# Threshold attention and a hard-swish projection on one core: both attention products of a quad end in one slot, and the last 64 keys are transposed by VectorE from 32 by 32 blocks

## Chip, cores and metric

The kernel runs on one core of a Trainium2 chip. Times are device microseconds of one execution. Five engines work side by side, each in its own fixed order of instructions: TensorE (PE, with its weight loads as PEld), VectorE (DVE), ScalarE (ACT), GpSimd (POOL) and SyncE (SP), which here only issues transfers.

## The reference

For each of 8 batches and 8 heads, with 576 tokens of 64 numbers:

```python
scores = scale * q @ k.T
thresh = max(scores) - tau                      # per row
scores = where(scores >= thresh, scores, -1e9)
attn = exp(scores - max(scores)); attn /= sum(attn) + 1e-9
x = attn @ v                                    # heads side by side: 4608 x 512
h = x @ w_in                                    # 512 -> 2048
out = (h * clip(h + 3, 0, 6) / 6) @ w_out       # 2048 -> 512
```

All inputs and the output are float32.

## The kernel before

**Tiling.** Two heads form a pair and four a quad; there are 16 quads. The 576 query rows of a head are four tiles of 128 and a rest of 64. A quad has 9 slots: slots 0 to 3 are the tiles of its first pair, 4 to 7 those of its second, and slot 8 has the rests of all four heads. The loop walks 144 slots in an order written out by hand (the scheduler is off), so what each engine does next is the order of these lines.

**A slot.** `scores` of a slot were issued at the end of the slot before, as 8 or 16 float32 matmuls into the two buffers of `ps_s` (tile `s` in the profile). VectorE takes the row maximum and moves the scores to SBUF (`sm_max`, line 277), GpSimd makes the bias (280), ScalarE masks (285) and exponentiates (290, one slot later), VectorE makes the reciprocal (293), GpSimd normalises to bf16 `pn` (298), and SP transposes `pn` by DMA to `pT` (slots 0 to 7) or `pR` (slot 8).

**Work put between.** To fill TensorE each slot also carries pieces of the projections of an earlier batch. `mm1` makes a piece of h (8 matmuls of width 256 or 320, line 353) in the single buffer of `ps_h`; its ReLU runs on ScalarE in slots 0, 1, 3, 5 (line 362) and on VectorE in the others (364), then VectorE's gate (370) writes `g`. Slot 8 has no `mm1`. `mm2_part` runs 4 of the 16 matmuls of an output tile (382, tile `o` in the single buffer of `ps_o`); every fourth part is followed by VectorE's eviction to `osb` (390) and a transfer. There is one part in each slot, none in slot 3, and two in slot 0 or 1.

**Attention products.** `av_main` (10 matmuls of width 512, lines 323 and 326, tile `av`) makes x for a pair from `pT`: for the first pair of a quad in slot 8, for the second in slot 3 of the next quad. `av_rest` (20 matmuls of width 64, tile `ar`) does the rest rows of a quad from `pR` in slot 4 of the next. Both end with a VectorE cast into `xT` (335, 343). Their PSUM bank comes from `bank`, which from slot 28 on always gives the single buffer of `ps_m`, shared with the transposes `tp` and `tr`.

**Keys and queries.** From the third batch on (quads 4 to 15) queries are loaded in 32 by 32 blocks and VectorE transposes them (222). Keys 0 to 511 are transposed by TensorE (213) and copied out by ScalarE (203). The last 64 keys of a quad's four heads lie in `kr`, loaded by two DMAs (107) in slot 6 for the quad after next; in slot 7 `transpose_rest` transposes them with one matmul (231, tile `tr`), and ScalarE moves the two halves to `kT`. Loads for a quad (`km`, `nq`, `kr`) leave SP's queue one step a slot in slots 4 to 8, between the DMA transposes.

Of the kernel before, what the change touches and what calls it, by code (L numbers as in the profile page):

```python
# [21 lines left out]
def kernel(  # L22
# [57 lines left out]
    def load_quad(quad):  # L80
        b, g = divmod(quad, 2)
        nat[quad] = (nat_pool.tile([P, 1152], F32, tag="nq", name="nq"),
                     nat_pool.tile([P, 4, 4, D], F32, tag="km", name="km"),
                     nat_pool.tile([P, 2 * D], F32, tag="kr", name="kr"))
        nq, km, kr = nat[quad]

        def main(dst, src, h, order):
            nc.sync.dma_start(out=dst[:, :, h, :], in_=src[b, 4 * g + h, 0:512, :].rearrange(order, t=4))

        def blocks_q(n, a, j):  # L90
            c = 32 * (2 * a + j)
            nc.sync.dma_start(out=nq[c:c + 32, n * S:(n + 1) * S].rearrange("p (k d) -> p k d", d=32),
                              in_=q[b, 4 * g + 2 * n + a, :, 32 * j:32 * j + 32].rearrange("(k r) d -> r k d", r=32))

        def load_q(n):
            if b < NB:
                for a in range(2):
                    main(nq[:, 0:1024].rearrange("p (t h d) -> p t h d", h=4, t=4), q, 2 * n + a, "(t p) d -> p t d")
            else:
                for a in range(2):  # L100
                    for j in range(2):
                        blocks_q(n, a, j)

        def rest():
            for dst, src in ((kr[:], k), (nq[:, 1024:1152], q))[0:2 if b < NB else 1]:
                for n in range(2):
                    nc.sync.dma_start(out=dst[64 * n:64 * n + 64, :].rearrange("p (h d) -> p h d", h=2),
                                      in_=src[b, 4 * g + 2 * n:4 * g + 2 * n + 2, 512:S, :].rearrange("h p d -> p h d"))

        for n in range(2):  # L110
            loads.append(lambda n=n: [main(km, k, 2 * n + a, "(p t) d -> p t d") for a in range(2)])
            loads.append(lambda n=n: load_q(n))
            if n == 0:
                loads.append(rest)
# [76 lines left out]
    def bank(name):  # L191
        nonlocal turn
        turn += 1
        if now < N2 and turn % 2:
            return ps_o.tile([P, 512], F32, tag="o", name=name)
        return ps_m.tile([P, 512], F32, tag="m", name=name)
# [29 lines left out]
        return lambda: copy_out(kT_of(pair)[:, 64:576], ps[:])  # L226

    def transpose_rest(quad):
        ps = bank("tr")
        nq, _, kr = nat[quad]  # L230
        nc.tensor.transpose(ps[:, 0:P], kr[:], identf[:])
        if by_pe(2 * quad):
            nc.tensor.transpose(ps[:, P:2 * P], nq[:, 1024:1152], identf[:])

        def evict():
            qT, kT = qkT[quad]
            both = ps[:].rearrange("p (w n t) -> p w n t", n=2, t=64)
            if by_pe(2 * quad):
                nc.vector.tensor_copy(out=qT[:, :, 512:S], in_=both[:, 1])
            copy_out(kT[0:64, :, S:S + 64], both[0:64, 0])  # L240
            copy_out(kT[64:P, :, 0:64], both[64:P, 0])
        return evict
# [66 lines left out]
    def pe_transpose(sl):  # L309
        ps = ps_h.tile([P, 2, 1024], BF16, tag="h", name="pt")  # L310
        ps = ps[:].rearrange("p a b -> p (a b)")[:, 0:2 * S].rearrange("p (c t) -> p c t", t=P)
        pn = sl.pn[:].rearrange("p a b -> p (a b)")
        for c in range(9):
            nc.tensor.transpose(ps[:, c, :], pn[:, c * P:(c + 1) * P], identb[:])
        return lambda: nc.vector.tensor_copy(out=sl.dst, in_=ps)
# [12 lines left out]
    def av_main(pair):  # L328
        b, hp = divmod(pair, NPAIR)
        if hp == 0:  # L330
            xT[b] = x_pool.tile([P, KI, S], BF16, tag="xT", name="xT")
        ps = bank("av")
        av(ps[:], pair, pts[pair], slice(0, 512))
        o0 = 64 if b % 2 else 0
        nc.vector.tensor_copy(out=xT[b][:, hp, o0:o0 + 512], in_=ps[:])  # L335

    def av_rest(quad):
        b, g = divmod(quad, 2)
        ps = bank("ar")
        for n in range(2):  # L340
            av(ps[:, n * 64:(n + 1) * 64], 2 * quad + n, ptr[quad], slice(n * 64, (n + 1) * 64))
        o0 = 0 if b % 2 else 512
        nc.vector.tensor_copy(out=xT[b][:, 2 * g:2 * g + 2, o0:o0 + 64],
                              in_=ps[:, 0:P].rearrange("p (a b) -> p a b", a=2))

    def mm1(item, pool=None):
        b, ni, c0, w = item
        hps = (pool or ps_h).tile([P, 2, 512], F32, tag="s" if pool else "h", name="h")  # L350
        for n in range(2):
            for ki in range(KI):
                nc.tensor.matmul(hps[:, n, 0:w], w_in_sb[:, ki, (ni + n) * P:(ni + n + 1) * P],  # L353
                                 xT[b][:, ki, c0:c0 + w], start=(ki == 0), stop=(ki == KI - 1))
        return hps[:, :, 0:w]
# [78 lines left out]
    for n, sl in enumerate(queue):  # L434
        quad, slot = sl.quad, sl.slot
        b, g = divmod(quad, 2)
        now = n
        if slot in (0, 4):
            pts[2 * quad + slot // 4] = pt_pool.tile([P, 9, 512], BF16, tag="pT", name="pT")
        if slot == 8:  # L440
            ptr[quad] = ptr_pool.tile([P, 9, P], BF16, tag="pR", name="pR")
        if quad == 0 and slot == 0:
            load_quad(1)
        if slot == (4 if quad else 8) and quad + 2 < NQUAD:
            load_quad(quad + 2)
        if slot == 0 and g == 1 and b + 1 < B:
            load_v(b + 1)
        if prev is not None:
            for i in range(2):
                sm_exp(prev, i)  # L450
        sm_max(sl)

        if slot != 8 and todo1:
            item, then = todo1.pop(0)
            h = mm1(item)
            r = mm1_relu(h, on_act=(slot in (0, 1, 3, 5)))
            mm1_gate(item, h, r)
            todo2.extend(then)
        copies = pe_transpose(queue[n - 2]) if n > 1 and queue[n - 2].on_chip else None
        if prev is not None:  # L460
            sm_recip(prev)
        if copies:
            copies()
        outs = []


        pieces = 0 if slot == 3 else 1
        if slot == 0:
            second = True
        if second and slot < 2 and len(todo2) > 1 and todo2[0][1] == todo2[1][1]:  # L470
            pieces, second = 2, False
        for _ in range(pieces):
            if todo2:
                bb, mt, part = todo2.pop(0)
                mm2_part(bb, mt, part)
                if part == 3:
                    outs += mm2_out(bb, mt, on_act=False)
        for i in range(2):
            sm_mask(sl, i)
        evict = None  # L480
        nxt = 2 * quad + 2
        if slot == (1 if quad else 2):
            evict = transpose_q(2 * quad + 1)
        elif slot == (2 if quad else 3):
            evict = transpose_k(2 * quad + 1)
        elif slot == 3 and quad > 0:
            av_main(2 * quad - 1)
        elif slot == 4 and quad > 0:
            av_rest(quad - 1)
            if quad % 2 == 0:  # L490
                todo1.extend(moe_of(quad // 2 - 1))
        elif slot in (5, 6, 7) and quad + 1 < NQUAD:
            if slot == 5:
                alloc_qk(quad + 1)
                evict = transpose_q(nxt)
            elif slot == 6:
                evict = transpose_k(nxt)
            else:
                evict = transpose_rest(quad + 1)
        elif slot == 8:  # L500
            av_main(2 * quad)
        if evict:
            evict()
        if n + 1 < len(queue):
            queue[n + 1].tiles = scores(queue[n + 1].quad, queue[n + 1].slot)
        if n < 8:
            warm_up(6)
        if prev is not None:
            sm_norm(prev)
        flush()  # L510
        late.extend(outs)
        start(loads, 1)
        if n < 4 or n > 12:
            start(vcasts, 1)
        if n > 3:
            start(casts, 1 if n < 24 else 2)
        prev = sl
# [24 lines left out]

    for item in todo1:
        rest1(*item)
    av_main(2 * last + 1)
    rest2()
    av_rest(last)
    for item in moe_of(B - 1):
        rest1(*item)
    rest2()  # L550
# [35 lines left out]
```

## Time and profile before

| What | us |
|---|---|
| Median of 8 runs | 562.63 (562.13 to 563.22) |
| Profiled execution | 562.28 |
| Its span | 560.5 |
| Quad 6, start to start of its scores | 30.12 |
| Quad 8 | 31.93 |
| Quad 13 | 32.68 |
| From the scores of the last slot to the end | 61.1 |

The span runs from the first to the last instruction of the profiled execution; the time of that execution has 1.8 us around it. The granted TensorE clock is 0.995 of full. Times in timelines count from the span's start. A line "A <- B" names the instruction that waited and what released it; "x8" counts merged instructions. Quads differ because of the widths of `mm1` and of where an output eviction falls.

### The profile page before, as it was taken

What the parts mean: (1) busy time and instruction counts of PE and PEld (TensorE: products, weight loads), DVE (VectorE), ACT (ScalarE), POOL (GpSimd) and SP (SyncE); (2) the same over time, 40 slices, a digit from 0 to 9 for tenths busy, and PEclk for the clock granted to TensorE, in tenths of its full rate; (3) what the DMA queues carried; (4) which work ended last, traced back from release to release, by engine and by line L of the source; (5) the groups of instructions that cost most, each with busy time, mean ns of one, the idle gap of its engine ahead of it and who ended that gap; (6) DMA issues with size and microseconds to landing.
All of it is one profiled execution on the core that took longest, in us unless ns stands there. A gap on an engine that the chain in (4) does not pass through costs nothing.

```text
span 560.5 us, 11593 instructions
## 1 busy us (share of the span) xinstructions
PE 530.4 (95%) x3815; PEld 308.4 (55%) x3856; DVE 424.4 (76%) x1040; ACT 470.0 (84%) x999; POOL 305.2 (54%) x646
## 2 busy tenths in 40 slices
PE   7898798799999999999999999999999999999997
PEld 5565355455555555655555555655555555654663
DVE  3687777687878798887978788887978788883440
ACT  3899899798888999899898999899888999983540
POOL 1878878864556555755556555754556555561000
PEclk9999899999999999999999999999999999999999
DMA  5989999986789877989699867977699866453102
GB/s 108 138 120 170 159 162 185 199 155 134 132 155 153 150 142 153 180 148 147 128 146 169 165 125 152 182 149 145 132 139 171 169 121 122 101 109 84 38 20 75
DMA packets 286204, 77.52 MB, mean 138 GB/s; under 512 B 269248, under 2 KB 281536, under 8 KB 286144
## 3 DMA queue, kind: packets, MB, share of 16 engines
q1 hardware_dynamic: 268736, 67.86, 65.5%
q0 software_dynamic: 17408, 8.92, 14.0%
q8 instruction: 30, 0.49, 0.4%
q14 instruction: 30, 0.25, 0.2%
HBM read 36.70 MB, written 9.44 MB: 82 GB/s over the span
## 4 chain that ended last, share of the span: by engine, by line
PE 55%; DVE 12%; ACT 10%; issue 4%; DMA 2%; SPq 2%; POOL 2%; DVEq 0%; POOLq 0%
PE h L353 17%; PE o L382 16%; PE s L256 15%; DVE s L277 5%; ACT s L285 4%; ACT s L290 3%; PE av L323 3%; DVE g L370 2%; DMA nq<-in_q_dram 2%; DVE r L364 2%; ACT r L362 2%; PE s L262 1%; PE tp L213 1%; POOL pn L298 1%; DVE osb L390 1%
## 5 line engine op out<-in xcount | busy, mean ns | idle before, releaser
L298 POOL TENSOR_SCALAR pn<-s,rinv 128x576 bf16<-128x576 f32 x288 | 211.6, 745 | 133.1 <-DVE rinv L293 58.4
L285 ACT ACTIVATE s<-s,bias 128x576 f32<-128x576 f32 x288 | 207.0, 766 | 35.7 <-POOL bias L280 34.6
L277 DVE TENSOR_SCALAR_CACHE_REDUCE s<-s 128x576 f32<-128x576 f32 x288 | 205.8, 752 | 40.4 <-PE s L256 30.5
L290 ACT ACTIVATE s<-s 128x576 f32<-128x576 f32 x288 | 192.7, 671 | 0.3
L256 PE MATMUL s<-kT,qT 64*128 64x288 f32 x1024 | 170.6, 430 | 5.9 <-DVE s L277 3.2
L353 PE MATMUL h<-xT,w_in_sb 128*128 128x320 bf16 (+1 forms) x1024 | 144.9, 287 | 5.9 <-DVE g L370 5.0
L382 PE MATMUL o<-w_out_sb,g 128*128 128x512 bf16 x535 | 133.5, 379 | 5.9 <-DVE osb L390 3.0
L353 PEld LDWEIGHTS <-w_in_sb 128*128 128x128 bf16 x1024 | 92.1, 97 | 68.8 <-issue 31.5
L256 PEld LDWEIGHTS s<-kT,qT 64*128 64x128 f32 x1024 | 93.9, 186 | 62.4 <-DVE s L277 24.9
L370 DVE SCALAR_TENSOR_TENSOR g<-r,h 128x512 bf16<-128x512 f32 (+1 forms) x128 | 96.4, 754 | 41.8 <-ACT r L362 39.9
L280 POOL TENSOR_SCALAR bias<-m 128x1 f32<-128x1 f32 x288 | 54.4, 189 | 67.6 <-DVE s L277 47.8
L382 PEld LDWEIGHTS <-g 128*128 128x128 bf16 x576 | 55.6, 98 | 58.2 <-issue 9.8
L362 ACT ACTIVATE r<-h,three 128x640 f32<-128x640 f32 (+1 forms) x74 | 54.4, 737 | 20.6 <-PE h L353 20.0
L290 ACT ACTIVATION_READ_ACCUMULATOR s<-s 128x1 f32 x288 | 54.2, 188 | 0.0
L364 DVE TENSOR_SCALAR r<-h 128x512 f32<-128x512 f32 (+1 forms) x54 | 40.5, 750 | 0.0
L390 DVE TENSOR_SCALAR osb<-o 128x512 f32<-128x512 f32 x31 | 21.0, 676 | 22.2 <-PE o L382 22.2
L323 PE MATMUL av<-pT,vm 128*64 128x512 bf16 x256 | 34.6, 393 | 2.1 <-ACT kT L203 2.0
L323 PEld LDWEIGHTS <-vm 128*64 128x64 bf16 x512 | 18.0, 111 | 25.3 <-issue 18.6
L293 DVE RECIPROCAL rinv<-rsum 128x2 f32<-128x2 f32 x144 | 23.0, 160 | 11.4 <-ACT s L290 10.1
L335 DVE CAST xT<-av 128x512 bf16<-128x512 f32 x32 | 21.8, 681 | 6.5 <-PE av L326 6.2
L277 DVE DVE_READ_ACCUMULATOR s<-s 128x1 f32 x288 | 23.9, 83 | 0.0
L388 ACT ACTIVATE osb<-o 128x512 f32<-128x512 f32 x5 | 3.0, 597 | 23.9 <-PE o L382 23.9
(42 smaller groups left out, 255.5 us busy)
## 6 DMA issues: line engine op xcount, KB each, us to landing
km<-in_k_dram SPq DMA_DIRECT2D x64, 128.0 KB, 3.1
out_dram<-osb SPq DMA_DIRECT2D x32, 256.0 KB, 2.4
nq<-in_q_dram SPq DMA_DIRECT2D x96, 72.0 KB, 2.9
vm<-in_v_dram POOLq DMA_DIRECT2D x16, 256.0 KB, 5.3
nq<-in_q_dram SPq DMA_DIRECT2D x16, 128.0 KB, 4.3
w_in_sb<-in_moe_w_in_dram POOLq DMA_DIRECT2D x16, 128.0 KB, 4.6
w_out_sb<-in_moe_w_out_dram POOLq DMA_DIRECT2D x16, 128.0 KB, 4.5
pT<-pn SPq DMA_TRANSPOSE x119, 3.4
```

What stands on the lines that cost most here:

```text
L256: nc.tensor.matmul(tiles[a][:, hf, 0:HALF], qT_of(pair)[a * 64:(a + 1) * 64, t * P:(t + 1) * P], keys(pair, a, hf), start=True, stop=True)
L277: nc.vector.tensor_scalar(out=sl.s[:, i, :].rearrange("p (a b) -> p a b", a=2), in0=ps[:, :, 0:HALF], scalar1=1.0, scalar2=None, op0=Alu.m ...
L280: nc.gpsimd.tensor_scalar(out=sl.bias[:, i:i + 1], in0=sl.m[:, i:i + 1], scalar1=-scale, scalar2=tau, op0=Alu.mult, op1=Alu.add)
L285: nc.scalar.activation(out=s, in_=s, func=Act.Prelu, bias=sl.bias[:, i:i + 1], scale=scale, alpha=REJECT)
L290: nc.scalar.activation(out=s, in_=s, func=Act.Exp, accum_out=sl.rsum[:, i:i + 1])
L298: nc.gpsimd.tensor_scalar(out=pn[:, i, :], in0=sl.s[:, i, :], scalar1=sl.rinv[:, i:i + 1], scalar2=1.0, op0=Alu.mult, op1=Alu.mult)
L323: nc.tensor.matmul(ps[a * 64:(a + 1) * 64, :], vm[:, 2 * hp + a, c * D:(c + 1) * D], pT[:, 5 * a + c, cols], start=(c == 0), stop=False)
L353: nc.tensor.matmul(hps[:, n, 0:w], w_in_sb[:, ki, (ni + n) * P:(ni + n + 1) * P], xT[b][:, ki, c0:c0 + w], start=(ki == 0), stop=(ki == KI ...
L362: nc.scalar.activation(out=r, in_=hps, func=Act.Relu, bias=three[:])
L364: nc.vector.tensor_scalar(out=r, in0=hps, scalar1=3.0, scalar2=0.0, op0=Alu.add, op1=Alu.max)
L370: nc.vector.scalar_tensor_tensor(out=gbuf[:, ni:ni + 2, c0:c0 + w], in0=r, scalar=6.0, in1=hps, op0=Alu.min, op1=Alu.mult)
L382: nc.tensor.matmul(o_ps[0], gbuf[:, ni, mt * P:(mt + 1) * P], w_out_sb[:, ni, :], start=(ni == 0), stop=(ni == NI - 1))
```

## The change

Four edits take effect together:

- From quad 3 on, `av_main` of the second pair moves from slot 3 to slot 4, and `av_rest` from the end of slot 4 to right behind it. Both stand ahead of the slot's `mm1`. `av_rest` no longer takes a bank of its own: it writes columns 384 to 511 of the second half of the buffer of `ps_h` that the same slot's `mm1` then fills in columns 0 to 255 or 0 to 319.
- The `mm2` part of slot 4 moves to slot 3, in the same quads.
- On VectorE the cast of `av` stands ahead of slot 4's ReLU, and the cast of `ar` behind its gate.
- In quads 4 to 15 `kr` is loaded in blocks by 8 DMAs of 32 partitions, and two VectorE transposes write the last 64 keys straight into `kT`; the matmul and ScalarE's two copies go.

```diff
+        def blocks_rest():
+            for a in range(2):
+                for j in range(2):
+                    c = 32 * (2 * a + j)
+                    for n in range(2):
+                        nc.sync.dma_start(
+                            out=kr[c:c + 32, 64 * n:64 * n + 64].rearrange("p (k d) -> p k d", d=32),
+                            in_=k[b, 4 * g + 2 * n + a, 512:S, 32 * j:32 * j + 32].rearrange("(k r) d -> r k d", r=32))
+
         def rest():
+            if b >= NB:
+                return blocks_rest()
...
     def transpose_rest(quad):
+        nq, _, kr = nat[quad]
+        if not by_pe(2 * quad):
+            kT = qkT[quad][1]
+            for a in range(2):
+                c = slice(64 * a, 64 * a + 64)
+                nc.vector.transpose(out=kT[c, :, S * (1 - a):S * (1 - a) + 64],
+                                    in_=kr[c, :].rearrange("p (n t) -> p n t", t=64))
+            return None
         ps = bank("tr")
...
-        nc.vector.tensor_copy(out=xT[b][:, hp, o0:o0 + 512], in_=ps[:])
-
-    def av_rest(quad):
+        return lambda: nc.vector.tensor_copy(out=xT[b][:, hp, o0:o0 + 512], in_=ps[:])
+
+    def av_rest(quad, ps=None):
         b, g = divmod(quad, 2)
-        ps = bank("ar")
+        ps = bank("ar") if ps is None else ps
...
+        evicts = []
+        both = quad > 2 and slot == 4
+        hps = None
+        if both:
+            hps = ps_h.tile([P, 2, 512], F32, tag="h", name="h")
+            evicts.append(av_main(2 * quad - 1))
+            evicts.append(av_rest(quad - 1, hps[:, 1, 384:512]))
         if slot != 8 and todo1:
             item, then = todo1.pop(0)
-            h = mm1(item)
+            h = mm1(item, hps=hps)
+            if both:
+                evicts.pop(0)()
             r = mm1_relu(h, on_act=(slot in (0, 1, 3, 5)))
             mm1_gate(item, h, r)
             todo2.extend(then)
+        for evict in evicts:
+            evict()
...
-        pieces = 0 if slot == 3 else 1
+        pieces = 0 if slot == (4 if quad > 2 else 3) else 1
...
-        elif slot == 3 and quad > 0:
-            av_main(2 * quad - 1)
+        elif slot == 3 and 0 < quad < 3:
+            evict = av_main(2 * quad - 1)
         elif slot == 4 and quad > 0:
-            av_rest(quad - 1)
+            if not both:
+                evict = av_rest(quad - 1)
```

More of the change, by code (lines that the diff above doesn't have):

```diff
@@ L228, in transpose_rest @@
     def transpose_rest(quad):
+        nq, _, kr = nat[quad]
[6 more added lines that the diff above has]
+            return None
         ps = bank("tr")
-        nq, _, kr = nat[quad]
         nc.tensor.transpose(ps[:, 0:P], kr[:], identf[:])
@@ L342, in av_rest, with mm1 @@
         o0 = 0 if b % 2 else 512
-        nc.vector.tensor_copy(out=xT[b][:, 2 * g:2 * g + 2, o0:o0 + 64],
-                              in_=ps[:, 0:P].rearrange("p (a b) -> p a b", a=2))
-    def mm1(item, pool=None):
+        return lambda: nc.vector.tensor_copy(out=xT[b][:, 2 * g:2 * g + 2, o0:o0 + 64],
+                                             in_=ps[:, 0:P].rearrange("p (a b) -> p a b", a=2))
+    def mm1(item, pool=None, hps=None):
         b, ni, c0, w = item
-        hps = (pool or ps_h).tile([P, 2, 512], F32, tag="s" if pool else "h", name="h")
+        if hps is None:
+            hps = (pool or ps_h).tile([P, 2, 512], F32, tag="s" if pool else "h", name="h")
         for n in range(2):
@@ L500 @@
         elif slot == 8:
-            av_main(2 * quad)
+            evict = av_main(2 * quad)
         if evict:
@@ L544 @@
         rest1(*item)
-    av_main(2 * last + 1)
+    av_main(2 * last + 1)()
     rest2()
-    av_rest(last)
+    av_rest(last)()
     for item in moe_of(B - 1):
```

## The prediction

> **What bounds the kernel now.** I read the page's busy line first, then the window view for single quads, then the timeline around the slots that change. (A quad is 9 slots; q13 s4 is slot 4 of quad 13.)
>
> ```profile
> PE 530.4 (95%) x3815; PEld 308.4 (55%) x3856; DVE 424.4 (76%) x1040; ACT 470.0 (84%) x999; POOL 305.2 (54%) x646
> ```
>
> ```profile
> core 0: us, PE busy (x) PEld busy (x) DVE busy (x) ACT busy (x) POOL busy (x), PEclk, DMA share, GB/s
> 190.18:220.30 30.12, 29.93 (x228) 17.56 (x229) 25.53 (x64) 28.07 (x62) 16.28 (x36) 1.00 0.79 146
> 345.97:377.68 31.71, 30.88 (x229) 17.98 (x230) 26.12 (x65) 28.90 (x63) 19.47 (x41) 1.00 0.95 169
> ```
>
> The rows are quad 6 and quad 11: window, its length, busy us of each engine. Quad 6 is TensorE from end to end; ScalarE fills 28.1 of 30.1 us and VectorE 25.5. Quad 11 (second) loses about 0.8 us to waits. So from quad 4 on, a step is worth its issue time on TensorE, plus any wait it makes or removes there. The next view, TensorE's timeline of q8 s3 and s4, prices the moved pieces from start to next start: av 1.20 (265.36 to 266.56), scores 1.17, h 1.31 when o follows and 1.19 when av follows (264.17 to 265.36), ar 0.44 (269.78 to 270.22).
>
> ```profile
> 265.36 1.05 PE L323 MATMUL av<-pT,vm 128*64 128x512 bf16 x8
> ...
> 266.56 1.24 PE L256 MATMUL s<-kT,qT 64*128 64x288 f32 x8
> 267.73 1.26 PE L353 MATMUL h<-xT,w_in_sb 128*128 128x320 bf16 x8
> 269.04 0.81 PE L382 MATMUL o<-w_out_sb,g 128*128 128x512 bf16 x3
> 269.78 0.32 PE L323 MATMUL ar<-pR,vm 128*64 128x64 bf16 x8
> ...
> 270.22 1.24 PE L256 MATMUL s<-kT,qT 64*128 64x288 f32 x8
> ```
>
> The wait that matters stands in q13 s4. The h bank is single. ScalarE's ReLU ran late, VectorE's gate ended at 425.86, and TensorE, waiting, began the next h 0.06 us later:
>
> ```profile
> 425.04 0.82 DVE L370 SCALAR_TENSOR_TENSOR g<-r,h 128x640 bf16<-128x640 f32 x1 [1.54 <-ACT r L362]
> ...
> 425.92 0.57 PE L353 MATMUL h<-xT,w_in_sb 128*128 128x320 bf16 x3 [0.44 <-DVE g L370]
> ```
>
> **What the Trainium skill says.** "Perfetto Trace Analysis", Identifying the Most-Contended Engine: matmul busy time does not measure how near TensorE is to its limit. I agree and use start-to-start steps. "TensorE: Matmul & The Clock Gate", Part 4: a transpose by TensorE takes about 275 ns inside a kernel; the records here say 273, but pipelined it advances the chain by only 0.11. "VectorE: DVE Perf Modes", The TRN2 errata: a fixed term of about 150 cycles at 0.96 GHz; for 576 elements (150+576)/0.96 = 756 ns, and the row below (from the groups by form) has 760. "DMA: Bandwidth & Descriptors", Specifications: under 512 B a transfer misses line rate. Pieces of kr go from 256 to 128 B, so both are under; no run here yet shows the small ones.
>
> ```profile
> L222 DVE STREAM_TRANSPOSE qT<-nq 128x576 f32<-128x576 f32 x24 | 18.2, 760 | 0.0
> ```
>
> **The change, part by part.**
>
> 1. Transpose of the last 64 keys, quads 4 to 15. One TensorE transpose leaves slot 7; the chain of waits in order of time has it at q8 s7:
>
> ```profile
> 280.60 0.11 PE tr L231
> 280.71 1.13 PE s L262 x16
> ```
>
> 12 x 0.11 = **-1.3 us**, on the path. ScalarE loses two copies of 252 ns a quad; it isn't the bound (28.1 of 30.1), so nothing. VectorE gains two 64-partition block transposes of 128 elements, not in the trace: an estimate by the page's fixed term, (150+128)/0.96 = 290 ns, about 0.21 each start to start, since VectorE operations overlap by 0.08; so 0.43 a quad. In q8 s8 VectorE idles 0.2 before its maximum, and the maximum ends 0.5 before the scores that need its bank: cover 0.7, cost nothing. With that cover gone, 12 x 0.43 = +5; below nothing excluded, it only adds to VectorE.
>
> 2. Loads of kr: 8 issues instead of 2, 6 more x 632 ns (median of an issue in the view of tile kr) = 3.8 us of SP a quad. Behind them on SP stand the pT transposes of slots 6 and 7, pR of slot 8, and km and nq of the quad after next. In q8 to q9 pR was issued at 290.0; with the backlog about 293.7, plus its median landing of 4.8: 298.5. av_rest wants it about 2.4 us into q9 s4, at 300.9. Cover 2.4, cost nothing. The pn buffers (4) come free a slot or so before they are wanted.
>
> 3. The reorder, quads 3 to 15. Slot 3 swaps av (1.20) for o (0.86); slot 4 swaps o for av. By the steps above slot 3 plus slot 4 stay 7.2 us: nothing. What is unknown is the changeover: av to scores now carries some 0.2 that av to ar may not, and ar to h needs a weight load of 97 ns. Bounds -0.2 and +0.1 a quad; I take -0.1: 13 x 0.1 = **-1.3 us**.
>
> 4. The new wait. In slot 4 the first projection now ends just before the scores of slot 5, and the next h waits until VectorE has read this bank out: ReLU (slot 4's is VectorE's), gate, and now the ar eviction, which reads the same buffer.
>
> ```profile
> 269.28 0.82 DVE L364 TENSOR_SCALAR r<-h 128x640 f32<-128x640 f32 x1
> 270.13 0.82 DVE L370 SCALAR_TENSOR_TENSOR g<-r,h 128x640 bf16<-128x640 f32 x1
> 270.87 0.16 DVE L293 RECIPROCAL rinv<-rsum 128x2 f32<-128x2 f32 x1
> ...
> 271.54 0.28 DVE L343 CAST xT<-ar 128x128 bf16<-128x128 f32 x1
> ```
>
> These rows are q8 s4. From the start of slot 5's scores: ReLU at 0.11 (ScalarE's ReLU of q8 s3 starts that long after the step that follows its h), gate 0.85 later, ar 0.74 after that, its 0.28, release 0.06: 2.04. The scores cover 1.17. Stall 0.87 at width 320. At width 256 (0.72 and 0.61 instead): 1.78 - 1.17 = 0.61. Slot 4 is 320 wide in quads 4, 5, 8, 9, 12, 13 and 256 in 3, 6, 7, 10, 11, 14, 15: 6 x 0.87 + 7 x 0.61 = **+9.5 us**. Bounds: 0.3 without the ar eviction; 1.2 if VectorE comes late. Queued behind that h are slot 5's o and the scores of slot 6. On VectorE the reciprocal comes some 1.7 us later, and GpSimd's norm and the bias of slot 5 behind it; that bias lands about 3.8 us into slot 5, ScalarE's own ReLU holds it to 4.1: hidden.
>
> 5. Waits that go. With mm2 in slot 3, the bank wait for the gate in s4 (q13 0.5, q9 0.15) goes, since av stands ahead of it. Quads 4 and 5 lose about 0.7 each, because the output eviction that delays the maximum in s2 comes a slot later; quad 3 about 0.8. Together **-2.9 us**. The shift comes about thus: in quad 3 slot 3 the second projection's list is empty, so one part slips and ends in the tail (0.86 less in the slots, 0.86 more there: nothing), and every later output eviction falls a slot later.
>
> 6. That shift elsewhere. Quads 3, 4, 5, 9, 13 now wait 0.6 to 0.9 at the start of slot 8:
>
> ```profile
> 313.69 0.59 PE L382 MATMUL o<-w_out_sb,g 128*128 128x512 bf16 x2 [0.53 <-DVE osb L390]
> ```
>
> These 3.3 go; quads 6, 10, 14 get the same wait, 3 x 0.75 = 2.2; quads 8 and 12 get the eviction in s5 before a block transpose, which delays the gate of s6: 2 x 0.55; quads 7 and 11 lose part of theirs, 2 x 0.3. Together -3.3 + 2.2 + 1.1 - 0.6 = **-0.6 us**.
>
> Sum: -1.3 - 1.3 + 9.5 - 2.9 - 0.6 = +3.4. The profiled execution took 562.28 (span 560.5 and 1.8 around it), 0.35 under the median 562.63; on the median it makes **566.0**.
>
> **Rivals.**
> - The pause lets the late engines catch up, and it costs little (faster, 0.20). Place: h of slot 5. Slots 0 to 8 of quads 3 to 15 hold about 12 us over the pure TensorE steps (quad 3 about 4, quads 4, 5, 13 about 1.7 each, 7 and 11 about 1). I return 6 or 7 of these; if all go, 9.5 - 1.3 - 1.3 - 12 = -5: 557.5. It decides from 8 returned. For it: ScalarE is late in quads 3, 7 and 11. Against: several of those waits follow an output eviction, which only moves.
> - VectorE becomes the bound of slots 5 to 8 (0.13): the delay of item 4 and the two transposes leave the maximum late, +0.4 in 12 quads: 566.0 + 5 = 571. For: in q10 VectorE starts it only 0.2 to 0.4 early in s6 and s7. Against: the stall of TensorE gives VectorE time too.
> - SP holds pR up (0.05): over 2.4 us late, av_rest and h behind it wait, perhaps 0.7 a quad, 12 x 0.7: 574. Against: SP waits for GpSimd most of the time.
> - That the reorder doesn't take place is excluded: the built order on TensorE has av, ar, h before the scores in slot 4 of quads 3 to 15.
>
> **How the numbers follow.** No change that can be told is about 0.2%, 1.1 us. My forecast has 0.62, of which 0.07 falls within that; the first rival 0.20, of it 0.05 within; the slower two 0.18. Slower 0.55 + 0.18 = 0.73, the same 0.12, faster 0.15. The range runs from half of the first rival's gain to the second rival's full cost: 560.5 to 572.
>
> **What would show it.** Right: h of slot 5 idle 0.6 to 0.9 with VectorE's xT eviction from h as releaser, 13 times; slot 7 shorter by 0.11; osb waits at slot 8 in quads 6, 10, 14. Wrong: no such gap, or gaps before the scores of slots 6 to 8 larger than it; pR as a releaser of TensorE would mean SP.

## The result, and the profile after

| | us |
|---|---|
| Before, median of 31 runs | 562.77 (561.37 to 566.20) |
| After, median of 11 runs | 573.37 (569.17 to 577.28) |
| Ratio | 1.0185, 95% interval 1.0164 to 1.0206 |
| Profiled execution of after | 569.17; span 567.4, mean granted clock 0.993 |

The change is slower, as forecast, but by 10.6 us where I had said 3.4, and outside my range by 1.4.

The busy line of the page of after: TensorE has a little less to do than before and takes longer over it.

```profile
PE 528.5 (93%) x3802; PEld 307.8 (54%) x3844; DVE 430.8 (76%) x1064; ACT 463.8 (82%) x975; POOL 305.3 (54%) x646
```

The window view of after, quad 6 and quad 11 (window, length, busy us of each engine, TensorE clock, DMA):

```profile
core 0: us, PE busy (x) PEld busy (x) DVE busy (x) ACT busy (x) POOL busy (x), PEclk, DMA share, GB/s
189.09:220.18 31.09, 29.76 (x228) 17.59 (x229) 26.71 (x68) 28.37 (x61) 16.75 (x37) 1.00 0.79 147
350.43:381.97 31.54, 30.50 (x228) 17.43 (x229) 26.16 (x65) 27.72 (x60) 19.05 (x40) 1.00 0.93 158
```

Quad 6, which had no gap, is 0.97 us longer; quad 11, which had gaps, is 0.17 shorter. The view of waits of after says what opened (engine, what waited, what released it: us together, times, longest):

```profile
PEld L372 <- DVE xT L361: 13.5, 12, 1.3
...
PE h L372 <- DVE xT L361: 8.3, 13, 0.8
...
PEld L341 <- DMA pR<-pn: 7.4, 6, 2.9
...
PE h L341 <- DMA pR<-pn: 4.7, 4, 2.4
```

Two new waits. The first pair (line 372 is mm1's matmul, 361 the cast of av_rest into xT) is the one I priced: 13 times, at most 0.8. The second pair I had at nothing: TensorE stands before av_rest (341) until the DMA transpose of the rests, pR, has landed. A weight load and its matmul wait for the same thing, so the two rows of a pair overlap and are not added.

The first wait in TensorE's and VectorE's timeline, after, q8 s5 (start, busy us, engine, line, in brackets the idle time before):

```profile
272.55 1.24 PE L274 MATMUL s<-kT,qT 64*128 64x288 f32 x8
...
272.66 0.82 DVE L383 TENSOR_SCALAR r<-h 128x640 f32<-128x640 f32 x1 [0.57 <-PE h L372]
...
273.51 0.82 DVE L389 SCALAR_TENSOR_TENSOR g<-r,h 128x640 bf16<-128x640 f32 x1
...
274.25 0.28 DVE L361 CAST xT<-h 128x128 bf16<-128x128 f32 x1
...
274.60 0.58 PE L372 MATMUL h<-xT,w_in_sb 128*128 128x320 bf16 x3 [0.81 <-DVE xT L361]
```

ReLU, gate and cast stand as I chained them: h starts 274.60 - 272.55 = 2.05 us after the scores (I had 2.04), and 1.17 of it is covered.

The second wait, in TensorE's timeline of after at q7 s4:

```profile
235.68 0.38 PE L344 MATMUL av<-pT,vr 128*64 128x512 bf16 x2
237.93 0.32 PE L341 MATMUL h<-pR,vm 128*64 128x64 bf16 x8 [1.86 <-DMA pR<-pn]
```

Its cause is on SP. First SP's timeline of before, then of after, both from slot 8 of quad 6 on (count at the end):

```profile
218.10 1.32 SPq L107 DMA_DIRECT2D kr<-in_k_dram  x2
...
227.54 3.38 SPq L306 DMA_TRANSPOSE pR<-pn  x1
```

```profile
217.73 4.97 SPq L109 DMA_DIRECT2D kr<-in_k_dram  x8
222.79 1.30 SPq L324 DMA_TRANSPOSE pT<-pn  x1
...
231.51 2.92 SPq L324 DMA_TRANSPOSE pR<-pn  x1
```

The eight loads hold SP 4.97 us instead of 1.32, 3.65 more. GpSimd had finished the rests at 225.65; their transpose is issued at 231.51, 5.86 after that (before: 1.51 after), and lands at 237.88. Of the 4.35 that it leaves later, 3.65 are the eight loads; the four issues of nq, which stand between them and pR, take 3.55 instead of 2.27. TensorE was through with av_main, and would have begun av_rest, at 235.9.

### The profile page after: what moved, and what is told of

It is laid out like the page before. It is cut to its first block, busy times and chain, and to the rows that moved or that the text cites. A ratio compares the mean times of both kernels' runs of the same rounds, so it can differ in the third digit from the quotient of the medians.

```text
span 567.4 us, 11661 instructions
## 1 busy us (share of the span) xinstructions
PE 528.5 (93%) x3802; PEld 307.8 (54%) x3844; DVE 430.8 (76%) x1064; ACT 463.8 (82%) x975; POOL 305.3 (54%) x646
```

## The experiments

**How they are compared.** Besides medians against before, I use the time from the scores of quad 4 to the end of the span in each profiled execution: the granted clock is 1.00 there (130 to 550 us) in all ten traces, while the first 125 us hold drops of it that differ from one execution to the next.

| Kernel | Median | Ratio to before (95%) | Quad 4 to end | against before |
|---|---|---|---|---|
| before | 562.8 | | 435.13 | |
| after | 573.37 | 1.0185 (1.0164 to 1.0206) | 441.92 | +6.8 |
| after_again | 569.56 | 1.0116 (1.0085 to 1.0148) | 440.60 | +5.5 |
| order_only | 565.54 | 1.0053 (1.0024 to 1.0082) | 439.05 | +3.9 |
| keys_only | 563.89 | 1.0017 (0.9997 to 1.0037) | 434.59 | -0.5 |
| spread | 564.86 | 1.0033 (1.0018 to 1.0047) | 438.14 | +3.0 |
| split8 | 565.81 | 1.0049 (1.0029 to 1.0070) | 436.61 | +1.5 |
| half_burst | 564.60 | 1.0044 (1.0027 to 1.0062) | 438.11 | +3.0 |
| keys_spread | 560.92 | 0.9976 (0.9962 to 0.9990) | 433.63 | -1.5 |
| rest_in_5 | 559.71 | 0.9953 (0.9930 to 0.9976) | 432.95 | -2.2 |

The theory: the new order costs the wait in slot 5; the eight loads cost nothing by themselves but make SP late with pR. The rival: the new keys or the order cost something else, VectorE's time above all.

**The order alone**

Against after, the last 64 keys are loaded and transposed as before:

```diff
         def rest():
-            if b >= NB:
-                return blocks_rest()
...
     def transpose_rest(quad):
-        if not by_pe(2 * quad):
...
-            return None
         ps = bank("tr")
```

> The changed order and the shared bank, but the last 64 keys loaded by two DMAs and transposed by TensorE as in the kernel before. Theory (two causes: h of slot 5 waits for VectorE's reads of the h bank, 0.61 or 0.87 us a quad; and pR lands late because six more loads stand ahead of it on SP): the wait of slot 5 stays at 0.61 and 0.87, no wait of TensorE for pR, slot 7 longer by 0.11; 564 to 566 us. Rival (pR is late only because av_rest asks for it about 1 us earlier): the waits for pR stay, some 5 us, and the time is 570 or more.

Measured 565.54. The slot 5 wait is there in full (8.3 us in 13 waits of h). One wait for pR is left, in quad 3, where the view of waits has

```profile
PE h L323 <- DMA pR<-pn: 1.1, 1, 1.1
```

I had expected none. From quad 4 on there is none, so what the order costs there, 3.9 us net, it costs without pR: the gaps of slot 5 (8.9 from start to start), less what other slots give back.

**The keys alone**

Against before, the same lines are added, and nothing else:

```diff
         def rest():
+            if b >= NB:
+                return blocks_rest()
...
     def transpose_rest(quad):
+        if not by_pe(2 * quad):
...
+            return None
         ps = bank("tr")
```

> The kernel before with the block loads of kr and VectorE's transposes alone. Theory: in the kernel before pR landed 2.4 us ahead of its use in quads 6 and 10 and 1.7 in quad 2; with 6 more loads ahead it comes about 4 us later, so ar of quads 3, 7 and 11 waits 1.5 to 2 us each, about 5 us together, against 1.3 saved on TensorE: 565 to 567. Rival (only the earlier demand makes pR late): no wait for pR, 561.3 us.

Measured 563.89, lower than expected, and not told from before (the interval holds 1). The view of waits shows pR all the same, in the old order too, and in the three quads named:

```profile
PE ar L341 <- DMA pR<-pn: 3.8, 3, 1.9
```

Slot 4 takes 5.71, 4.03 and 4.96 us in quads 3, 7 and 11, where before it took 3.70, 3.55 and 3.55. Part of it is paid back: slots 6 and 7 of quads 7 and 11 fall from 7.95 us to 7.28, as if TensorE's pause let the other engines catch up, and TensorE has 12 transposes less.

**The change with its loads spread out**

```diff
-        def blocks_rest():
-            for a in range(2):
-                for j in range(2):
+        def blocks_rest(a, j):
...
         def rest():
-            if b >= NB:
-                return blocks_rest()
...
-            if n == 0:
+            if n == 0 and b < NB:
                 loads.append(rest)
+        if b >= NB:
+            for a in range(2):
+                for j in range(2):
+                    loads.append(lambda a=a, j=j: blocks_rest(a, j))
```

Against after: the same eight DMAs leave two a slot, in slots 8, 0, 1 and 2, and the second km and nq of a quad, which stood behind them, leave a slot earlier. Engines other than SP do what they do in after.

> The changed kernel with the eight loads of kr issued two a slot in four slots (8, 0, 1, 2) behind the other loads, not eight in one slot. Theory: the waits for pR (5.9 us in the trace of the changed kernel) go, the wait of slot 5 stays at 0.61 and 0.87: 563 to 565 us. Rival (the time lies in VectorE's transposes or in the order, not in SP's queue): 571 or more.

Measured 564.86. TensorE waits for pR nowhere; the slot 5 wait stays. Waits of spread:

```profile
PE h L372 <- DVE xT L361: 9.2, 14, 0.9
```

In SP's timeline at quad 6, the transpose of pR is no longer behind the loads; it leaves 0.96 us after GpSimd:

```profile
223.81 0.93 SPq L107 DMA_DIRECT2D kr<-in_k_dram  x2
224.84 1.28 SPq L324 DMA_TRANSPOSE pR<-pn  x1
226.16 1.13 SPq L107 DMA_DIRECT2D kr<-in_k_dram  x2
```

Against after, all that spread saves from quad 3 on lies in four quads: 1.56 us in quad 3, 3.03 in 7, 0.38 in 9, 0.40 in 11. Quads 6, 10 and 14 take 31.09 in both. What the burst costs in the profiled execution of after is thus 5.4 us: 3.8 at full clock, and quad 3's 1.6, which is less sure, since the clock from 90 to 130 us was 0.96 in after and 1.00 here.

Against order_only, which differs in the keys, spread gains 0.11 in quads 4, 5, 7, 9, 11 and 13. In 6, 10 and 14 it gains nothing: at slot 8 TensorE waits for the output eviction anyway. In 8 and 12 it loses 0.12, because the two block transposes push VectorE's maximum of the slot 8 before past the next scores. Spread, at the end of quad 7:

```profile
247.61 0.62 DVE L245 STREAM_TRANSPOSE kT<-kr 64x128 f32<-64x128 f32 x2
...
248.95 0.75 DVE L295 TENSOR_SCALAR_CACHE_REDUCE s<-s 128x576 f32<-128x576 f32 x1
...
249.53 1.47 PE L274 MATMUL s<-kT,qT 64*128 64x288 f32 x8
```

These scores, which need the banks that the maximum reads, take 1.47 instead of the 1.24 of order_only, where the maximum ends 0.52 before they start.

**Eight loads without the block keys**

Against before, `kr` of quads 4 to 15 comes in 8 plain DMAs of 16 partitions:

```diff
         def rest():
+            if b >= NB:
+                for n in range(2):
+                    for i in range(4):
+                        nc.sync.dma_start(out=kr[64 * n + 16 * i:64 * n + 16 * i + 16, :].rearrange("p (h d) -> p h d", h=2),
+                                          in_=k[b, 4 * g + 2 * n:4 * g + 2 * n + 2, 512 + 16 * i:528 + 16 * i, :].rearrange("h p d -> p h d"))
+                return
```

> The kernel before, with kr of quads 4 to 15 loaded in the same layout but as eight DMAs of 16 partitions in the same slot; TensorE transposes as before. Theory (SP's queue): waits of ar for pR as in keys_only, 1.5 to 2 us in quads 3, 7, 11; 566 to 568. Rival (VectorE's transposes cost the time, not the loads): 562.8, no change.

Measured 565.81, at the low edge. The waits are those of keys_only, with the keys still transposed by TensorE:

```profile
PE ar L329 <- DMA pR<-pn: 2.5, 3, 1.1
```

Here a late pT also holds av up, once each in quads 3 and 11 (5.1 us together). So the number of issues on SP does it, not the blocks, nor VectorE. That this kernel is slower than keys_only fits the 12 transposes on TensorE that it keeps, the later pT, and lower clock in its first 130 us; I did not part these.

**Half the burst**

Against after, four loads stay in slot 6 and four go to slot 0 of the next quad, behind pR:

```diff
-        def blocks_rest():
-            for a in range(2):
+        def blocks_rest(half=0):
+            for a in (half,):
...
+        if b >= NB:
+            loads.append(lambda: blocks_rest(1))
```

> The changed kernel with four of the eight kr loads left in slot 6 and the other four issued in slot 0, behind pR: two more loads than before stand ahead of pR, not six. Theory (pR's lateness is the backlog of SP): pR is issued about 2.5 us earlier than in the changed kernel, its waits all but go, 565 to 567 us, between the spread loads (564.9) and the changed kernel (573.4). Rival (any more loads disturb the transfers themselves): as many loads, so 570 or more.

Measured 564.60, a little under what I had expected. No wait for pR is left; it is issued 1.44 us (quad 6) and 2.38 (quad 10) after GpSimd and has 2.57 and 1.35 us to spare. Four loads are as good as two a slot: up to there the queue's backlog lies inside pR's slack and costs nothing.

**The change again, with a second profile**

The kernel of after without an edit: its profiled execution had been the shortest of its runs, and I wanted to see where a longer one is longer.

> The changed kernel once more, unaltered, since its first profile (569.2) was its quickest run. Theory: a run near the median of 573 has more waits for pR, 9 to 12 us together against 5.9, and the same 0.61 and 0.87 at slot 5. Rival (the spread comes from TensorE's clock or from elsewhere): the waits for pR stay near 6 us while the span is about 572.

This one took 574.19. The theory that the longer runs hold more waits for pR fell:

```profile
PE h L341 <- DMA pR<-pn: 3.9, 3, 1.8
```

That is less than the 4.7 of the first. From quad 4 on it is even 1.3 us shorter. It loses its time before: quad 4 starts at 131.78 instead of 125.47. The window view of it from 90 to 130 us, and then that of the first profile of after:

```profile
90.00:130.00 40.00, 34.62 (x232) 20.00 (x230) 26.92 (x70) 32.33 (x70) 27.09 (x57) 0.87 1.13 171
```

```profile
90.00:130.00 40.00, 33.99 (x237) 20.04 (x240) 28.66 (x73) 34.15 (x73) 26.66 (x56) 0.96 1.14 163
```

The granted clock (third number from the right) is 0.87 where it had been 0.96, and 0.89 in the first 30 us where it had been 1.00. TensorE gets through fewer instructions there. That is the rival that I had put beside it.

**The keys alone, spread**

keys_only, with the edit of spread:

```diff
+        if b >= NB:
+            for a in range(2):
+                for j in range(2):
+                    loads.append(lambda a=a, j=j: blocks_rest(a, j))
```

> The kernel before with VectorE's transposes and the kr loads two a slot in slots 8, 0, 1, 2. Theory: TensorE saves 0.11 in 12 quads, no wait for pR: 561.4, 1.0 to 1.5 under the kernel before. Rival (VectorE's transposes cost 0.3 or more a quad): 563 to 566.

Measured 560.92: faster than before, and no wait of TensorE for pR. So this part of the change was good and its burst alone spoiled it. That it gains 1.5 us from quad 4 on, close to item 1's 1.3, is partly luck. Quads 4 to 15 gain 1.1: slot 7 is 0.11 shorter in quads 4 to 14, but in 4, 5 and 9 the wait for the output eviction at slot 8 grows by as much, and in 13 slot 8 is 0.24 shorter too. The other 0.4 lies behind TensorE's last matmul (from its start to the end 4.06 us instead of 4.43), and split8, which keeps TensorE's transposes, has it too (4.08).

**The rests in slot 5**

Against spread, av_main of slot 4 stands behind mm1, and av_rest goes to slot 5, behind its mm1 and mm2 part, in a bank of `ps_m`:

```diff
-        if both:
-            hps = ps_h.tile([P, 2, 512], F32, tag="h", name="h")
-            evicts.append(av_main(2 * quad - 1))
-            evicts.append(av_rest(quad - 1, hps[:, 1, 384:512]))
...
         elif slot == 4 and quad > 0:
+            if quad > 2:
+                evict = av_main(2 * quad - 1)
...
+        if slot == 5 and quad > 2:
+            evict_r = av_rest(quad - 1)
```

The mm2 part stays in slot 3. The first projections of a new batch, which read av_rest's rows, become due in slot 5 too.

> The mm2 part in slot 3, av_main behind mm1 in slot 4, av_rest in its own bank in slot 5, block keys with spread loads. Theory (the wait of slot 5 comes from mm1 standing last in slot 4): no wait of 0.6 to 0.9 in slot 5, pR wanted a slot later than before, and the shorter slot 7, the vanished waits of slots 3, 4 and 8 are kept: 557 to 559 us. Rival (the gains of the changed kernel hang on the pause that the wait gives to VectorE and ScalarE): waits come back elsewhere, 562 to 565.

Measured 559.71, 0.7 above the expectation, but faster than before and after, and nearer to the theory than to the rival. TensorE's timeline, q8 from the scores of slot 5 on:

```profile
266.46 1.24 PE L274 MATMUL s<-kT,qT 64*128 64x288 f32 x8
267.64 1.26 PE L372 MATMUL h<-xT,w_in_sb 128*128 128x320 bf16 x8
268.73 1.03 PE L401 MATMUL o<-w_out_sb,g 128*128 128x512 bf16 x4
269.69 0.32 PE L341 MATMUL ar<-pR,vm 128*64 128x64 bf16 x8
```

h follows the scores at 1.18, without a gap. Yet from quad 4 on the kernel is only 5.2 us shorter than spread, whose slot 5 waits hold 8.9 there by start-to-start times. And not all of the 5.2 is theirs: since the new projections become due a slot later, quad 4 has no piece of h in slot 5. It gives 1.52 with a gap of 0.87, while the stretch from the last scores to the end, where that piece now falls, is only 0.30 longer. Quad 9 gives 0.55 in slots 4 and 5 where its gap was 0.88; quad 10 gives 0.47 in all where the gap was 0.61. Quads 8 and 12 pay 0.58 again in slot 6, where VectorE has the output eviction, a query transpose and the cast of av_rest in a row, and get 0.39 of it back in slot 7. The 0.1 to 0.3 that are short in quads 9 and 10 lie in other changeovers between kinds of matmul; which of them I did not separate.

## Why the prediction was wrong, point by point

- **Item 1, the transpose: right.** Slot 7 went from 3.34 to 3.23 and from 3.12 to 3.01 (0.11 each). VectorE's block transpose takes 301 ns by the view of tile kr, where the Trainium skill ("VectorE: DVE Perf Modes", The TRN2 errata) gave my estimate of 290. Two of them take 0.63 us a quad, not 0.43, since they do not overlap. "Cover 0.7, cost nothing" held in the old order (keys_spread), but not everywhere in the new one: in quads 8 and 12 the first scores take 0.22 longer (see spread). And where TensorE waits at slot 8 for the output eviction, the 0.11 only makes that wait longer, so the 12 x 0.11 do not all arrive.
- **Item 2, the loads: this step failed.** The size was right (3.65 against 3.8 us of SP). "Cover 2.4, cost nothing" was not. I followed one transfer, quad 8's into quad 9, and let it land after the median of all pR transfers, 4.8. In the trace of before that very transfer took 7.62 to land; 290.0 + 3.7 + 7.6 = 301.3 was past the 300.9 wanted, by 0.4. Quad 9's slot 4 in after is 0.38 longer than in spread. (That the two agree is partly luck: counted from the quad's start, pR left 3.0 later, not 3.7, and was wanted 0.5 earlier than 300.9, in part because slot 3 is 0.34 shorter by item 3's own steps.) And it was not the tightest: the same trace gives the time between landing and first use. Off it ("less both") go 3.65 for the loads and 0.83 (slot 4 at width 256) or 0.94 (320), because av_rest moved ahead of mm1 and mm2. The next two columns are measured, from the start of the quad that uses pR: how much later pR was issued in after than in before, and how much earlier av_rest was due (before to spread, where nothing waits for pR):

| pR of quad | to spare before | less both | issued later | wanted earlier | to spare after |
|---|---|---|---|---|---|
| 2 | 1.69 | -2.8 | 1.8 | 1.8 | none (TensorE waits) |
| 6 | 2.37 | -2.1 | 4.1 | 1.1 | none |
| 10 | 2.47 | -2.0 | 3.7 | 1.1 | none |
| 8 | 4.21 | -0.4 | 3.0 | 1.5 | none |
| 4 | 5.32 | 0.7 | 3.1 | 1.9 | 0.48 |
| 12 | 5.64 | 1.1 | 2.2 | 1.9 | 0.93 |

  All six signs come out, and every other quad keeps at least 0.7 by this working, so it finds the transfers in danger. Their sizes it does not give: av_rest is wanted earlier by more than slot 4 alone explains, because slot 3 is shorter and waits went, and with 1.9 in place of 0.94 quad 4 would stand at -0.3, where 0.48 was left. What is below zero adds up to 7.3 us, more than the 5.4 that after lost to it in its profile, for one thing because pR of quad 10 landed in 4.7 us that time instead of 6.7. With 7.3 in place of nothing the forecast would have been 573.3; that this meets the median of 573.37 is chance.
- **The rival that came true had 0.05.** I dismissed SP with "SP waits for GpSimd most of the time". In the trace of before its transposes wait 246.5 us of 560.5 for GpSimd, which is less than half, and not between slots 6 and 8; a queue's mean idle time says nothing of a burst. My price, 0.7 in each of 12 quads, was wrong in its shape: nothing in nine quads, 0.4 to 3 in four from quad 3 on. That its total, 574, lies next to the measured 573.4 is luck.
- **Item 3, the reorder: right.** Slots 3 and 4 of quad 8 together: 7.22 before, 7.11 after; -0.11.
- **Item 4, the new wait: right** as a gap, 0.88 at width 320 and 0.61 at 256, in 13 quads. rest_in_5 shows that removing these gaps is worth less than their sum.
- **Item 5, waits that go: right.** Slots 2 to 4 of quad 4: 11.27 to 10.50; quad 13's slots 3 and 4: 7.81 to 7.11, with item 3's share in it.
- **Item 6, the shift: right but for two quads.** Slot 8 of quads 3, 4, 5, 9, 13 is 3.30 again. In quads 6, 10, 14 it is 0.69 longer (I had 0.75), with the output eviction as releaser: after, quad 6, VectorE and TensorE:

```profile
217.30 0.67 DVE L409 TENSOR_SCALAR osb<-o 128x512 f32<-128x512 f32 x1
...
218.03 1.02 PE L401 MATMUL o<-w_out_sb,g 128*128 128x512 bf16 x3 [0.63 <-DVE osb L409]
```

  In quads 8 and 12 it cost 0.39 in slot 7, item 1 apart, not 0.55. Quads 7 and 11 gained 0.95 each, item 1 apart, not 0.3: their slots 6 and 7 had 7.95 us and have 6.89. Before, VectorE had the output eviction in slot 6 right ahead of a query transpose and the maximum (quad 7):

```profile
242.21 0.67 DVE L390 TENSOR_SCALAR osb<-o 128x512 f32<-128x512 f32 x1
242.79 0.77 DVE L222 STREAM_TRANSPOSE qT<-nq 128x576 f32<-128x576 f32 x1
243.49 0.72 DVE L277 TENSOR_SCALAR_CACHE_REDUCE s<-s 128x576 f32<-128x576 f32 x1
```

  In spread and in rest_in_5 that eviction comes a slot later. Late engines catching up in the pause, the first rival's mechanism, may have a part in it, but not the main one: rest_in_5, which has no gap in slot 5 of these quads, still gains 0.76 of the 0.95.

**The sum.** In quads 4 to 15 my items without SP make about +4.4; spread, which has all of them and no wait for pR, measures +2.0 there. Of the 2.4 between, 1.3 are quads 7 and 11, and most of the rest is 0.15 to 0.2 in each of quads 6, 8, 10, 12, 13 and 14. The stretch from the last scores to the end is 0.96 longer, near the 0.86 of the part that slips there, which makes up the +3.0 of the table. After adds 3.8 to spread from quad 4 on, and 1.6 in quad 3.

**What stays open.** After's profiled execution is 6.9 us longer than before's (569.17 against 562.28); its median is 4.2 above that execution. Over 83 runs of before, the time rises by 2.9 us for each 0.01 that the mean clock is lower; after's runs have a median of 0.991 and before's 0.994, which makes about 0.9. The longer profile of after puts its loss into the first 130 us and not into pR. But the runs of after, after_again, keys_only and split8, which have three or four waits for pR, scatter more about such a line (standard deviation 1.7 to 2.1 us) than those of the others (0.6 to 1.1), so part of the rest may be pR too, in runs that left no trace. Taken to equal clock by that line, after's runs lie 9.1 us above before in the first comparison and 5.5 in the second, and spread's 2.6. By whole runs the burst thus costs 6.5 or 2.9 us; the 5.4 of the one trace lies between. And after's own median was 573.37 in one comparison and 569.56 in the other, from no cause that I can show.

## What to carry to other kernels

A step that adds issues to a queue is priced by the slack of every transfer behind it: landing to first use, each with its own landing, the tightest first, never by a median landing or the queue's mean idle time. Take off at once what the same change does to the consumer: here the loads held SP 3.65 us longer and the order called for pR 1.1 to 1.9 us earlier. keys_only has three of the waits and order_only one; all four came only with both together. When loads are cut into more pieces, issue them a few a slot, behind the transfer that somebody is waiting for. Two products in one PSUM bank tie the next user to the slower reader; that gap is easily foreseen, and giving the small product a slot of its own brought back only about half of it.

## What I had not expected of the hardware

- The same DMA transpose, pR, takes 3.2 to 3.6 us from issue to landing for the odd quads 5 to 13 in the trace of before, and 5.2 to 8.4 for the even ones from 2 to 12. Behind the even ones, V loads are issued on GpSimd's queue (from 225.98 on in the trace of before, for quad 6). That these cause it was not tried. Nor does the trace settle how much the loads on SP matter: quads 6 and 10 take 7.2 and 6.7 in before, 5.2 and 4.9 in spread, and 6.4 and 4.7 in after, whose burst is the largest.
- A DMA issue on SP was shorter for the smaller loads: median 0.43 us for one of the eight loads of kr, 0.63 for one of the two. In split8, whose eight loads keep the pieces of 256 B, it is 0.42, so the size of a piece is not what made it shorter. Eight still take nearly four times as long as two (4.97 against 1.32 us), since some 0.2 us stand between them.
- The granted clock is 1.00 from 130 us on in every trace, and falls to 0.87 to 0.96 in some stretches before that, not the same ones in each execution.
